# A fused retention and two-MoE kernel: the first batch's retention ordered by hand, one converted pair of weights ahead of the products

## The chip, the cores and the metric

The kernel runs on one core of a Trainium2 chip. The metric is device time in microseconds of one execution, the median of the runs shown. The engines are TensorE (PE, matrix products into PSUM), VectorE (DVE), ScalarE (ACT), GpSimd (POOL) and SyncE (SP, which issues the loads). Each works through its own queue in order.

## The reference

Three operators in a row: a retention with decay over 4 batches of 768 tokens with 8 heads of 64, a dense MLP with a squared ReLU (512 to 2048 to 512), and a mixture of 8 experts whose tokens are assigned by a greedy sort of the gate's logits. Only the first two bear on the change:

```
def _attn_ref(q, k, v):
    gamma = 1.0 - 2.0 ** (-5.0 - np.arange(H))
    for t in range(S):
        state = gamma[None, :, None, None] * state + np.einsum('bhd,bhe->bhde', k[:, :, t], v[:, :, t])
        y[:, :, t] = scale * np.einsum('bhd,bhde->bhe', q[:, :, t], state)

def _moe_ref(x, w_in, w_out, s, b):
    h = x @ w_in
    r = np.maximum(h, 0.0)
    return (s * (r * r) + b) @ w_out
```

## The kernel before

**Retention in chunks.** A chunk is 128 tokens of a batch; a batch has six (`CPB`), a block `blk` is two of them. Four tiles of a chunk are loaded (`load_chunk`: q and k by feature, k and v by token, 256 KB each) and a tile of decay factors (`load_dec`). `scale_chunk` multiplies q and v by their decays, for the first batch on POOL but for chunk 0's q. The retention of chunk j has two parts. `b_part` (here: the score step) multiplies k by q for all heads into two PSUM banks, L328, and DVE multiplies the result by the causal mask into `am`, L334. `c_part` (the value step) adds three products: `am` by v, L348, the state's update k by v, L354, and q by the state before it, L358. ACT then copies the result to `xh` (L366), DVE writes the rest to `xl` (L367), and ACT copies the state from PSUM into `Sbd` (L373), which the next chunk's value step reads. Value steps of the first four blocks write banks 5 and 2 in turn.

**High and low halves.** Every large product is made of three with operands split into a high and a low float: weights h and l, activations xh and xl, rh and rl.

**Conversion.** The dense MLP's weights come as 64-bit words. `conv_gen` turns a raw tile into a pair f of weights (its W_in part, h and l number 2f, and its W_out part, number 2f + 1), sixteen pairs in all. For a pair, ACT takes the magnitude (L237) and copies the high halves (L258), and DVE does nine operations: L248, L250, L253, L261, L263, and for both halves a subtraction L268 and an addition L270 that writes l. A raw tile is loaded two pairs ahead into one of two buffers (`conv_load`, L230), when the pair two before is done.

**Products.** For pair f and block, an h unit (`h_unit`, L415) is twelve products into bank 2 or 3 in turn; ACT takes ReLU (L418), square and high half; DVE writes the low half `rl` (L434, `low_parts`) when the next h unit is emitted. An x unit (`x_unit`, L444) is six products that add to the block's output, emitted two units behind. `moe1` runs three blocks of the first batch together: 48 h units and 48 x units in turn.

**What sets the order.** The code is emitted by hand, and each engine's queue has the order in which it is emitted. In the first stage two generators compete: `attn3` (three blocks of retention) and the conversion, by due times that the generators yield; the conversion's are stretched by `PRO` = 1.5 until pair `PN` = 2 is ready, so two pairs are ready when the products start. In the product stage `Weave` emits the product units at a fixed cost each (1,320 and 1,300) and lets the conversion go on where its due time has come: 7,100 for a pair. `conv_until(f)` emits what is missing of a pair before its first h unit.

**Then** come the retention of block 3, products of blocks 3 to 11 one after another with the next block's retention between them, and the expert stage.

Of the kernel before, what the change touches and what calls it, by code (L numbers as in the profile page):

```python
# [81 lines left out]
def kernel(  # L82
# [14 lines left out]
    x2_scratch=None,  # L97
    log_out=None,
    stages=2,
    PRO=1.5,  # L100
    PN=2,
    CY=(700, 1200, 650),
    SY=(3200, 3800, 3200, 2500, 2200, 800),
    IY=(600, 1800, 800),
# [4 lines left out]
    WARM=24,  # L109
# [65 lines left out]
    def load_chunk(j):  # L175
        if j < CPB:

            ts = []
            for i in range(4):
                n = 2 * NF - 1 - 2 * j - i // 2  # L180
                tag = ("h", "l")[i % 2] + str(n)
                ts.append(wpool.tile([128, 512], F32, name=f"first{j}_{i}", tag=tag))
            for i in (0, 1, 3, 2):
                SP.dma_start(ts[i], qkv[j, :, i])
                if j == 0 and i in first:
                    first[i]()
            if j:
                load_dec(j)
        else:
            ts = []  # L190
            load_dec(j)
            t = loads.tile([128, 4, 512], F32, name="q")
            for i in (0, 2):
                SP.dma_start(t[:, i:i + 2], qkv[j, :, i:i + 2])
                ts += [t[:, i, :], t[:, i + 1, :]]
        QKV[j] = ts

    def scale_chunk(j, q=POOL, v=POOL):
# [3 lines left out]
        if v:  # L202
# [6 lines left out]
    wb = bank(3)[:, 0:TB]  # L209
    DVE.memset(warm, 0.0)  # L210
    nv = CPB * n0
    first = {0: lambda: load_dec(0),
             1: lambda: SP.dma_start(mask_f[:, 0:128], cst[:, 128:256]),
             3: lambda: SP.dma_start(vdec, dec[:, nv:nv + CPB * H].rearrange("p (a b) -> p a b", b=H))}
    load_chunk(0)
    DVE.tensor_copy(mask, mask_f[:, 0:128])
# [15 lines left out]
    def conv_gen():  # L232
        mag = {}

        def magnitude(f):
            mag[f] = stage.tile([128, 1024], F32, name="c", tag="sa")
            ACT.activation(mag[f], RAW[f].bitcast(F32).rearrange("p (n t) -> p t n", t=2)[:, 1, :], AF.Abs)  # L237

        magnitude(0)
        for f in range(NF):  # L240
            raw = RAW.pop(f)
            (_, hi), (_, hf), (lo, _), (lf, _) = (
                [v[:, t, :] for t in range(2)] for v in
                (raw.bitcast(d).rearrange("p (n t) -> p t n", t=2) for d in (I32, F32, U32, F32)))
            c = mag.pop(f)
            ci = c.bitcast(I32)

            DVE.tensor_scalar(c, c, ZERO_WORD, None, op0=OP.max)  # L248
            yield CY[0]
            DVE.tensor_scalar(ci, ci, 3, 0x3FFFFFFF, op0=OP.logical_shift_left, op1=OP.bitwise_and)  # L250
            yield CY[0]

            DVE.scalar_tensor_tensor(hi, hi, -0x40000000, ci, op0=OP.bitwise_and, op1=OP.bitwise_or)  # L253
            for i in range(2):
                n = 2 * f + i
                W[n] = (wpool.tile([128, 512], F32R, name=f"h{n}", tag=f"h{n}"),
                        wpool.tile([128, 512], F32R, name=f"l{n}", tag=f"l{n}"))
                ACT.activation(W[n][0], hf[:, i * 512:(i + 1) * 512], AF.Copy)  # L258
            yield CY[1]

            DVE.tensor_scalar(ci, hi, -0x800000, None, op0=OP.bitwise_and)  # L261
            yield CY[0]
            DVE.scalar_tensor_tensor(lf, lo, 2.0 ** -52, c, op0=OP.mult, op1=OP.mult)  # L263
            yield CY[1]
            for i in range(2):
                h, l = W[2 * f + i]
                part = slice(i * 512, (i + 1) * 512)
                DVE.tensor_tensor(hf[:, part], hf[:, part], h.bitcast(F32), op=OP.subtract)  # L268
                yield CY[2]
                DVE.tensor_tensor(l, hf[:, part], lf[:, part], op=OP.add)  # L270
                if f + 1 < NF and not i:
                    magnitude(f + 1)
                yield CY[2]
            if f + 2 < NF:
                conv_load(f + 2)
            READY.add(f)
# [4 lines left out]
    XF = []  # L281
    pST = [None]

    def attn(blk, wide):

        if blk == NB - 1:

# [29 lines left out]
        def b_part(j):  # L317
# [17 lines left out]
                                  mask[:, None, :].to_broadcast([128, NP, 128]), op=OP.mult)  # L335
            am_of[j] = am

        def c_part(j):
            c = c0 + j
            if wide:  # L340
# [18 lines left out]
                              skip_group_check=True)  # L359
            js = slice(j * 128, (j + 1) * 128)  # L360
            yv = py.rearrange("p (a b) -> p a b", b=128)
            if blk == NB - 1:
                for i in range(2):
                    ACT.activation(XF[i][:, :, js], yv[:, 2 * i:2 * i + 2], AF.Copy, scale=scale)
            else:
                ACT.activation(xh[:, :, js], yv, AF.Copy, scale=scale)  # L366
                DVE.scalar_tensor_tensor(xl[:, :, js], yv, scale, xh[:, :, js].bitcast(F32), op0=OP.mult,  # L367
                                         op1=OP.subtract)
            if c < CPB - 1:
                pv = pST[0][:, 0:NP * 64].rearrange("p (a b) -> p a b", b=64)  # L370
                for s in range(2):
                    ss = slice(s * 64, (s + 1) * 64)
                    ACT.activation(Sbd[ss, :, ss], pv[ss], AF.Copy)  # L373
            ch = 2 * blk + j + 2
            if CPB + 2 <= ch < NC:
                load_chunk(ch)

        for j in range(2):
            if not wide:
                yield from scale_gen(j)  # L380
            yield from b_part(j)
            if wide:
                yield 1500
                if j:
                    c_part(0)
                    yield 2500
            else:
                yield 4500
                c_part(j)
                yield 9000  # L390
# [139 lines left out]
    def moe1(blks, xbs, lag, apart=0):  # L530
# [5 lines left out]
        for n in range(len(seq) + lag):  # L536
            if n < len(seq):
                def hu(n=n):
                    f, i = seq[n]
                    conv_until(f)  # L540
                    low_parts()
                    r = h_unit(blks[i], f, 2 + n % 2)
                    R2[blks[i], f] = r_split(r, work.tile([128, TB], F32R, name="rh", bufs=3),
                                             work.tile([128, TB], F32R, name="rl", bufs=3))
                units.append((1320, hu))
# [8 lines left out]
                units.append((1300, xu))  # L554
        return units

    conv_load(0)
    load_chunk(1)
    SP.dma_start(sb[:, 0:1], bass.AP(tensor=moe_s.tensor, offset=moe_s.offset, ap=[[0, 128], [1, 1]]))
    SP.dma_start(sb[:, 1:2], bass.AP(tensor=moe_b.tensor, offset=moe_b.offset, ap=[[0, 128], [1, 1]]))  # L560
    for j in range(2, CPB):
        load_chunk(j)
        if j == 3:
            conv_load(1)
    scale_chunk(0, DVE)

    def attn3():
        for b in range(3):
            yield from attn(b, True)

    a3 = Side(attn3())
    conv.due = 3000.0
    while not a3.done:
        if conv.due < a3.due and PN not in READY:
            t = conv.due
            conv.step()
            conv.due = t + PRO * (conv.due - t)
        else:
            a3.step()
    conv.due = 0.0  # L580
    wv = Weave([conv])
    for u in moe1((0, 1, 2), ((4, 5), (6, 7), (0, 1)), 2):
# [610 lines left out]
```

## Time and profile before

| | |
|---|---|
| median of 3 runs | 1068.57 us (1066.97 to 1070.48) |
| the profiled execution | 1078.43 us, its span 1076.7 us |
| PE busy | 1003.4 us, 93% of the span |
| DVE busy | 769.2 us, 71% |
| ACT busy | 462.7 us, 43% |
| POOL busy | 77.0 us, 7% |
| loads and stores | 104.48 MB, mean 97 GB/s |

The profile is of one execution on the one core. A busy share is a mean over stages with different limits, so the stages are read one by one. The granted clock is that of PE, 1.00 for the upper of its two levels (2.4 GHz) and 0.50 for the lower (1.2 GHz). A row of the timeline gives start, duration, engine, line, operation and tiles, how many in a row, and in brackets how long the engine had been idle and what ended that.

### The profile page before, as it was taken

What the parts mean: (1) busy time and instruction counts of PE and PEld (TensorE: products, weight loads), DVE (VectorE), ACT (ScalarE), POOL (GpSimd) and SP (SyncE); (2) the same over time, 40 slices, a digit from 0 to 9 for tenths busy, and PEclk for the clock granted to TensorE, in tenths of its full rate; (3) what the DMA queues carried; (4) which work ended last, traced back from release to release, by engine and by line L of the source; (5) the groups of instructions that cost most, each with busy time, mean ns of one, the idle gap of its engine ahead of it and who ended that gap; (6) DMA issues with size and microseconds to landing.
All of it is one profiled execution on the core that took longest, in us unless ns stands there. A gap on an engine that the chain in (4) does not pass through costs nothing.

```text
span 1076.7 us, 19597 instructions
## 1 busy us (share of the span) xinstructions
PE 1003.4 (93%) x7664; PEld 879.8 (82%) x7664; DVE 769.2 (71%) x1954; ACT 462.7 (43%) x1002; POOL 77.0 (7%) x99
## 2 busy tenths in 40 slices
PE   5699999899999999999998999889898988889997
PEld 4598888789899999999997987667687876768996
DVE  3799994478787787887744525869888988776431
ACT  1366664444444444344443651414433353424531
POOL 3200002000000000000000000011112021120211
PEclk8899999999999999999999999989898999999999
DMA  9234333422212121312121000522343342434430
GB/s 313 101 118 152 123 134 121 147 90 79 60 59 75 44 87 35 95 46 73 42 78 33 2 1 1 179 67 89 108 148 117 119 138 88 153 113 157 156 108 30
DMA packets 35036, 104.48 MB, mean 97 GB/s; under 512 B 4736, under 2 KB 5248, under 8 KB 34944
## 3 DMA queue, kind: packets, MB, share of 16 engines
q1 hardware_dynamic: 30528, 89.60, 25.3%
q0 software_dynamic: 3840, 12.59, 3.5%
q8 instruction: 60, 0.98, 0.4%
q10 hardware_dynamic: 576, 1.05, 0.3%
q14 instruction: 32, 0.26, 0.1%
HBM read 90.64 MB, written 12.58 MB: 96 GB/s over the span
## 4 chain that ended last, share of the span: by engine, by line
PE 65%; DVE 21%; issue 8%; DMA 2%; ACT 1%; POOL 1%; another core or an unknown queue 0%; SPq 0%; POOLq 0%; DVEq 0%; ACTq 0%
PE b L415 23%; PE b L444 18%; PE b L1023 6%; PE b L1044 4%; PE b L672 3%; DVE l L1004 3%; PE b L782 2%; PE b L348 2%; DVE big L918 2%; PE b L358 2%; DVE cmp L775 2%; PE b L328 2%; DVE hl L1032 1%; DVE raw L268 1%; DMA first<-in_qkv_dram 1%
## 5 line engine op out<-in xcount | busy, mean ns | idle before, releaser
L467 DVE SCALAR_TENSOR_TENSOR scr<-tmp,wg 128x512 bf16<-128x512 f32 x288 | 198.2, 688 | 8.8 <-ACT tmp L454 3.9
L415 PE MATMUL b<-xh,h 128*128 128x256 f32 x704 | 199.7, 284 | 1.5 <-DVE xls L367 1.4
L415 PE MATMUL b<-xl,h 128*128 128x256 f32 x704 | 199.4, 283 | 0.0
L415 PE MATMUL b<-xh,l 128*128 128x256 f32 x704 | 199.4, 283 | 0.0
L418 ACT ACTIVATE r<-b 128x256 f32<-128x256 f32 x192 | 73.3, 382 | 207.1 <-PE b L415 200.3
L415 PEld LDWEIGHTS b<-xh,h 128*128 128x128 f32 x704 | 134.7, 191 | 10.2 <-DVE xls L367 1.6
L415 PEld LDWEIGHTS b<-xl,h 128*128 128x128 f32 x704 | 134.7, 191 | 5.5
L415 PEld LDWEIGHTS b<-xh,l 128*128 128x128 f32 x704 | 134.7, 191 | 0.0
L444 PE MATMUL b<-h,rl 128*128 128x512 f32 x320 | 126.0, 394 | 3.4 <-DVE rl L434 3.4
L444 PE MATMUL b<-h,rh 128*128 128x512 f32 x320 | 128.9, 403 | 0.0
L444 PE MATMUL b<-l,rh 128*128 128x512 f32 x320 | 126.0, 394 | 0.0
L1023 PE MATMUL b<-gh,h 128*128 128x384 f32 x256 | 94.3, 368 | 9.4 <-DVE hl L1032 6.9
L434 DVE TENSOR_TENSOR rl<-r,rh 128x256 fp32r<-128x256 f32 x160 | 68.7, 430 | 46.3 <-ACT rh L427 46.0
L1023 PE MATMUL b<-gl,h 128*128 128x384 f32 x256 | 89.5, 349 | 1.5 <-DVE gl L968 1.5
L1023 PE MATMUL b<-gh,l 128*128 128x384 f32 x256 | 89.7, 351 | 0.0
L1004 DVE TENSOR_TENSOR l<-eraw,h 128x512 fp32r<-128x512 f32 x128 | 82.2, 683 | 0.0
L426 ACT ACTIVATE r<-r 128x256 f32<-128x256 f32 x192 | 79.8, 416 | 5.1
L1026 ACT ACTIVATE hh<-b 128x384 fp32r<-128x384 f32 x64 | 31.2, 488 | 117.8 <-PE b L1023 116.3
L1044 PE MATMUL b<-h,hh 128*128 128x512 f32 x192 | 79.6, 415 | 2.2 <-ACT hh L1026 2.2
L996 ACT ACTIVATE h<-eraw 128x512 fp32r<-128x512 f32 x128 | 72.7, 622 | 10.2 <-DMA eraw<-in_w_dram 9.8
L444 PEld LDWEIGHTS b<-h,rl 128*128 128x128 f32 x320 | 60.1, 188 | 20.4 <-DVE rl L434 7.1
L1044 PE MATMUL b<-h,hl 128*128 128x512 f32 x192 | 76.1, 396 | 0.4 <-DVE hl L1032 0.4
(193 smaller groups left out, 1825.4 us busy)
## 6 DMA issues: line engine op xcount, KB each, us to landing
eraw<-in_w_dram SPq DMA_DIRECT2D x64, 512.0 KB, 3.5
q<-in_qkv_dram SPq DMA_DIRECT2D x36, 512.0 KB, 4.9
raw<-in_w_dram SPq DMA_DIRECT2D x32, 512.0 KB, 4.2
first<-in_qkv_dram SPq DMA_DIRECT2D x24, 256.0 KB, 6.0
qdec<-in_dec_dram SPq DMA_DIRECT2D x24, 256.0 KB, 2.9
x2d<-tmp SPq DMA_DIRECT2D x20, 256.0 KB, 5.7
wg<-in_wgT_dram SPq DMA_DIRECT2D x4, 512.0 KB, 5.8
x2d<-tmp ACTq DMA_DIRECT2D x4, 256.0 KB, 2.3
```

The source lines that it names most:

```text
L415: PE.matmul(ph, a[:, ks], b[:, kc, :], start=(n == 0), stop=(n == 3 * KC - 1))
L418: ACT.activation(r, ph, AF.Relu)
L426: ACT.activation(r, r, AF.Square)
L434: DVE.tensor_tensor(rl, r, rh.bitcast(F32), op=OP.subtract)
L444: PE.matmul(X2[blk][t], a[:, ts], b, start=(f == 0 and i == 0), stop=(f == NF - 1 and i == 2))
L467: DVE.scalar_tensor_tensor(scr, x, 1.0, WG[e], op0=OP.mult, op1=OP.mult, accum_out=of[:, e:e + 1])
L672: PE.matmul(XB[c], a[:, cs], b, start=(f == 0 and i == 0), stop=(f == NF - 1 and i == 2))
L996: ACT.activation(hi, raw[:, a, :], AF.Copy)
L1004: DVE.tensor_tensor(lo, raw, hi.bitcast(F32), op=OP.subtract)
L1023: PE.matmul(PH[0], a[:, ks], b[:, kc, :], start=(kc == 0 and n == 0), stop=(kc == KC - 1 and n == 2))
L1026: ACT.activation(hh, PH[0], AF.Relu)
L1044: PE.matmul(Y[i, t], a[:, ts], b, start=(f == 0 and j == 0), stop=(f == NF2 - 1 and j == 2))
```

## The change

The first batch's retention is no longer given by competing generators; a loop written by hand emits it.

- The retention's body becomes a function of its own, `retention`, that returns the score and the value step. The score steps of chunks 0 and 1 come first, then for each chunk its value step, conversion steps, the score step of the chunk two ahead, more conversion steps. A table `FC` gives the number of conversion steps before and after the score step: 5 and 0, 1 and 1, 1 and 0, 1 and 0, then none. These nine are the whole of pair 0 but its end, so one pair is ready when the products start, not two; pair 1 is emitted from there on.
- Pair 1's magnitude is emitted at the end of pair 0, not within it.
- 24 filler products are added between the score steps of chunks 0 and 1.
- Loads: the decay tile is second in its chunk, not last; the first raw tile comes behind chunk 1, not before it; the second comes last, behind chunk 5.
- In the value step of blocks 0 to 3 (`wide`), the state is copied ahead of `xh`, not behind `xl`.
- h units begin with bank 3, not 2, in all blocks.

```diff
-    PRO=1.5,
-    PN=2,
+    FC=((5, 0), (1, 1), (1, 0), (1, 0), (0, 0), (0, 0)),
@@ load_chunk
             for i in (0, 1, 3, 2):
                 SP.dma_start(ts[i], qkv[j, :, i])
+                if i == 0:
+                    load_dec(j)
                 if j == 0 and i in first:
                     first[i]()
-            if j:
-                load_dec(j)
@@ conv_gen
-                if f + 1 < NF and not i:
+                if f and f + 1 < NF and not i:
                     magnitude(f + 1)
                 yield CY[2]
+            if f == 0:
+                magnitude(1)
@@ c_part
+            if wide:
+                state(c)
             if blk == NB - 1:
...
-            if c < CPB - 1:
-                pv = pST[0][:, 0:NP * 64].rearrange("p (a b) -> p a b", b=64)
-                for s in range(2):
-                    ss = slice(s * 64, (s + 1) * 64)
-                    ACT.activation(Sbd[ss, :, ss], pv[ss], AF.Copy)
+            if not wide:
+                state(c)
@@ moe1
-                    r = h_unit(blks[i], f, 2 + n % 2)
+                    r = h_unit(blks[i], f, 3 - n % 2)
@@ the first stage
+    load_chunk(1)
     conv_load(0)
-    load_chunk(1)
+    load_chunk(2)
...
-    for j in range(2, CPB):
+    for j in range(3, CPB):
         load_chunk(j)
-        if j == 3:
-            conv_load(1)
+    conv_load(1)
     scale_chunk(0, DVE)
-    def attn3():
-        for b in range(3):
-            yield from attn(b, True)
-
-    a3 = Side(attn3())
-    conv.due = 3000.0
-    while not a3.done:
-        if conv.due < a3.due and PN not in READY:
-            t = conv.due
+    rets = [retention(blk, True) for blk in range(CPB // 2)]
+
+    def scores(j):
+        for _ in rets[j // 2][1](j % 2):
+            pass
+
+    def convert(n):
+        for _ in range(n):
             conv.step()
-            conv.due = t + PRO * (conv.due - t)
-        else:
-            a3.step()
+
+    scores(0)
+    for _ in range(WARM):
+        PE.matmul(wb, warm[:, 0:128], warm, start=True, stop=True)
+    scores(1)
+    for j in range(CPB):
+        rets[j // 2][2](j % 2)
+        convert(FC[j][0])
+        if j + 2 < CPB:
+            scores(j + 2)
+        convert(FC[j][1])
     conv.due = 0.0
```

The order on the engines shows it at three places. First SP's queue behind chunk 0; firstj_0, _1, _3, _2 are chunk j's q, k, v and k by token, qdec its decay tile, raw a raw tile (two loads). Before:

```order
L230 DMA raw_135<-in_w64_dram 128x512 x2
L184 DMA first1_0_138<-in_qkv_dram 128x512
L184 DMA first1_1_139<-in_qkv_dram 128x512
L184 DMA first1_3_141<-in_qkv_dram 128x512
L184 DMA first1_2_140<-in_qkv_dram 128x512
L173 DMA qdec1_146<-in_dec_dram 128x512
```

And in the changed kernel:

```order
L183 DMA first1_0_135<-in_qkv_dram 128x512
L172 DMA qdec1_140<-in_dec_dram 128x512
L183 DMA first1_1_136<-in_qkv_dram 128x512
L183 DMA first1_3_138<-in_qkv_dram 128x512
L183 DMA first1_2_137<-in_qkv_dram 128x512
L228 DMA raw_145<-in_w64_dram 128x512 x2
```

The raw tile has moved behind chunk 1, and the decay tile to the second place.

Second, DVE's queue in the retention, from chunk 2's mask (am_301 before, am_302 now, two operations for a chunk) to chunk 3's low half; raw and c are pair 0's conversion. Before:

```order
L261 TENSOR_SCALAR c_249<-raw_135 128x1024
L263 SCALAR_TENSOR_TENSOR raw_135<-raw_135,c_249 128x1024
L334 TENSOR_TENSOR am_301<-b6_291,mask_72 128x512
L334 TENSOR_TENSOR am_301<-b7_292,mask_72 128x512
L334 TENSOR_TENSOR am_316<-b0_306,mask_72 128x512
L334 TENSOR_TENSOR am_316<-b1_307,mask_72 128x512
L268 TENSOR_TENSOR raw_135<-raw_135,h0_254 128x512
L270 TENSOR_TENSOR l0_255<-raw_135 128x512
L367 SCALAR_TENSOR_TENSOR xl_288<-b5_323,xh_287 128x4x128
```

And in the changed kernel:

```order
L246 TENSOR_SCALAR c_277<-c_277 128x1024
L248 TENSOR_SCALAR c_277<-c_277 128x1024
L251 SCALAR_TENSOR_TENSOR raw_145<-raw_145,c_277 128x1024
L259 TENSOR_SCALAR c_277<-raw_145 128x1024
L261 SCALAR_TENSOR_TENSOR raw_145<-raw_145,c_277 128x1024
L334 TENSOR_TENSOR am_302<-b6_292,mask_72 128x512
L334 TENSOR_TENSOR am_302<-b7_293,mask_72 128x512
L376 SCALAR_TENSOR_TENSOR xl_196<-b2_305,xh_195 128x4x128
L266 TENSOR_TENSOR raw_145<-raw_145,h0_282 128x512
L334 TENSOR_TENSOR am_343<-b0_333,mask_72 128x512
L334 TENSOR_TENSOR am_343<-b1_334,mask_72 128x512
L268 TENSOR_TENSOR l0_283<-raw_145 128x512
```

Five conversion operations stand together ahead of chunk 2's mask, and from there on one stands between a low half and the next mask.

Third, DVE's queue at the end of the product stage's conversions; l31 is the last low half of the weights, rl the low halves of the h units' results. Before:

```order
L263 SCALAR_TENSOR_TENSOR raw_1582<-raw_1582,c_1644 128x1024
L268 TENSOR_TENSOR raw_1582<-raw_1582,h30_1683 128x512
L434 TENSOR_TENSOR rl_1706<-r_1703,rh_1705 128x256
L270 TENSOR_TENSOR l30_1684<-raw_1582 128x512
L268 TENSOR_TENSOR raw_1582<-raw_1582,h31_1686 128x512
L270 TENSOR_TENSOR l31_1687<-raw_1582 128x512
L434 TENSOR_TENSOR rl_1735<-r_1732,rh_1734 128x256
```

And in the changed kernel:

```order
L261 SCALAR_TENSOR_TENSOR raw_1678<-raw_1678,c_1746 128x1024
L266 TENSOR_TENSOR raw_1678<-raw_1678,h30_1779 128x512
L268 TENSOR_TENSOR l30_1780<-raw_1678 128x512
L444 TENSOR_TENSOR rl_1809<-r_1806,rh_1808 128x256
L266 TENSOR_TENSOR raw_1678<-raw_1678,h31_1782 128x512
L268 TENSOR_TENSOR l31_1783<-raw_1678 128x512
L444 TENSOR_TENSOR rl_1838<-r_1835,rh_1837 128x256
```

The last rl ahead of l31 is the 38th of the stage before and the 41st now: ten h units' low halves follow l31 before, seven now. Behind this place the queues of all engines have the same order in both kernels, but for one ACT copy of `xh` in block 3.

## Rows read from the trace of the kernel before

**Rows 1.** Busy time by stretch: start:end, length, engines (instructions), PE's clock, DMA, GB/s.

```profile
7.00:54.00 47.00, 26.94 (x313) 23.58 (x313) 27.54 (x36) 12.84 (x23) 14.41 (x11) 0.78 0.58 207
...
102.00:167.80 65.80, 63.64 (x395) 54.66 (x393) 64.25 (x95) 42.03 (x91) 3.29 (x2) 1.00 0.40 137
```

**Rows 2.** The chain of waits, 0 to 62 us: start, duration, what.

```profile
43.78 1.23 DVE raw L253
```

**Rows 3.** Timeline of PE, 0 to 60 us: score, value and first h products.

```profile
7.06 1.16 PE L328 MATMUL b<-first,first 64*128 64x128 f32 x16 [0.69 <-DVE first L201]
...
16.10 2.08 PE L328 MATMUL b<-first,first 64*128 64x128 f32 x16 [7.87 <-DMA first<-in_qkv_dram]
...
18.11 1.97 PE L348 MATMUL b<-am,first 128*64 128x128 f32 x16
...
20.45 1.04 PE L348 MATMUL b<-am,first 128*64 128x128 f32 x16
...
21.56 0.69 PE L354 MATMUL b<-first,first 128*64 128x64 f32 x16
...
39.91 1.16 PE L358 MATMUL b<-first,sbd 128*128 128x128 f32 x8
...
45.67 0.43 PE L348 MATMUL b<-am,first 128*64 128x128 f32 x2 [2.62 <-DVE am L334]
...
47.99 2.08 PE L358 MATMUL b<-first,sbd 128*128 128x128 f32 x8
...
54.00 0.39 PE L415 MATMUL b<-xh,h 128*128 128x256 f32 x1 [1.41 <-DVE xls L367]
```

**Rows 4.** The chain of waits, 160 to 196 us.

```profile
166.52 1.19 DVE rl L434
...
168.95 1.42 PE b L415 x12
170.37 1.39 PE b L444 x6
...
194.22 1.14 PE b L328 x16
```

**Rows 5.** Timeline of DVE in the product stage: first and fourteenth pair's start, an rl.

```profile
55.19 0.69 DVE L248 TENSOR_SCALAR c<-c 128x1024 f32<-128x1024 f32 x1
...
59.26 0.42 DVE L434 TENSOR_TENSOR rl<-r,rh 128x256 fp32r<-128x256 f32 x1
...
159.95 0.69 DVE L248 TENSOR_SCALAR c<-c 128x1024 f32<-128x1024 f32 x1
```

**Rows 6.** Timeline of POOL, 0 to 40 us: scaling of chunks 1, 2 and 3.

```profile
14.79 1.26 POOL L201 TENSOR_TENSOR first<-first,qdec 128x512 f32<-128x512 f32 x1 [6.58 <-DMA qdec<-in_dec_dram]
...
19.46 1.27 POOL L201 TENSOR_TENSOR first<-first,qdec 128x512 f32<-128x512 f32 x1 [2.41 <-DMA qdec<-in_dec_dram]
...
23.04 1.49 POOL L201 TENSOR_TENSOR first<-first,qdec 128x512 f32<-128x512 f32 x1 [1.31 <-DMA qdec<-in_dec_dram]
```

**Rows 7.** Timeline of ACT and DVE, 0 to 60 us: copies, conversion operations, masks.

```profile
21.53 1.15 ACT L237 ACTIVATE c<-raw 128x1024 f32<-128x1024 f32 x1
...
23.44 1.64 DVE L250 TENSOR_SCALAR c<-c 128x1024 int32<-128x1024 int32 x1
...
25.12 1.95 DVE L253 SCALAR_TENSOR_TENSOR raw<-raw,c 128x1024 int32<-128x1024 int32 x1
...
30.28 2.17 DVE L263 SCALAR_TENSOR_TENSOR raw<-raw,c 128x1024 f32<-128x1024 uint32 x1
...
37.98 0.60 ACT L366 ACTIVATE xh<-b 128x512 fp32r<-128x512 f32 x1 [7.19 <-PE b L358]
38.47 0.77 ACT L373 ACTIVATE sbd<-b 64x256 f32<-64x256 f32 x2
...
44.93 2.48 DVE L334 TENSOR_TENSOR am<-b,mask 128x512 f32<-128x512 f32 x4
```

**Rows 8.** Raw tiles' loads in the product stage, issue to landing.

```profile
DMA to landing us min/median/max: 3.4/3.6/4.7
```

More of the change, by code (lines that the diff above doesn't have):

```diff
@@ L211 @@
     nv = CPB * n0
-    first = {0: lambda: load_dec(0),
-             1: lambda: SP.dma_start(mask_f[:, 0:128], cst[:, 128:256]),
+    first = {1: lambda: SP.dma_start(mask_f[:, 0:128], cst[:, 128:256]),
              3: lambda: SP.dma_start(vdec, dec[:, nv:nv + CPB * H].rearrange("p (a b) -> p a b", b=H))}
@@ L282, with retention @@
     pST = [None]
-    def attn(blk, wide):
+    def retention(blk, wide):
         if blk == NB - 1:
@@ L336, in b_part, with state @@
             am_of[j] = am
+        def state(c):
+            if c < CPB - 1:
+                pv = pST[0][:, 0:NP * 64].rearrange("p (a b) -> p a b", b=64)
+                for s in range(2):
+                    ss = slice(s * 64, (s + 1) * 64)
+                    ACT.activation(Sbd[ss, :, ss], pv[ss], AF.Copy)
         def c_part(j):
@@ L376, in c_part, with attn @@
                 load_chunk(ch)
+        return scale_gen, b_part, c_part
+    def attn(blk, wide):
+        scale_gen, b_part, c_part = retention(blk, wide)
         for j in range(2):
```

## The prediction

> **What bounds the kernel now.** The table by stretches comes first [rows 1]. From 7 to 54 us, where the first batch's retention runs, TensorE (PE) is busy 26.94 of 47.00 us at a mean granted clock of 0.78, and VectorE (DVE) 27.54: nothing is full, so latencies rule. From 102.0 to 167.8, in the product stage, DVE is busy 64.25 of 65.80 us: there DVE is the bound. The chain of waits of the first 62 us [rows 2] shows what the latencies are: conversion operations on DVE (43.78), and then the masks that stand behind them in its queue. The first product of the next stage, at 54.00, waited 1.41 us for DVE's low half xls [rows 3]. The chain of the product stage [rows 4] runs over DVE until the subtraction rl ends at 167.71, then over PE without a gap to 194.22. So the end of the stage is the start of DVE's conversions in it, plus DVE's work up to that rl, plus the products left then. One h unit takes 1.43 us and one x unit 1.39 [rows 4]; a pair of units 2.82.
>
> Below, S(j) are the score products of chunk j, V(j) its three value products, T_P is the start of the first h unit (54.00 before), T_D that of the first conversion operation DVE does after the last retention step (55.19 before [rows 5]).
>
> **Loads.** SP's queue gives bytes at fixed places: before, the decay tiles of chunks 1, 2 and 3 end at 3.76, 5.07 and 6.38 MB, and the scaling on POOL that waits for them starts at 14.79, 19.46 and 23.04 us [rows 6]. Now each decay tile stands second in its chunk and the first raw pair behind chunk 1: chunk 1's ends at 1.92 MB, chunk 2's at 4.28, chunk 3's at 5.60, the raw pair at 3.76. Between those marks (2.7 to 3.6 us for a MB) this gives about 10 us (half of the bytes that were there at 14.79), 16.7, 20.9, and 14.8 for the raw pair; on the same slope chunk 4's comes at 24.5 and chunk 5's at 28. These are estimates from the three rows.
>
> **Retention by hand.** S(0) is where it was (7.06 [rows 3]). The added 24 fillers cost 24 x 0.119 = 2.9 us at the upper clock level (an h unit is twelve such products in 1.43 us [rows 4]), 5.7 at the lower; they cover PE's wait for chunk 1, which is scaled at 10 + 1.3 = 11.3. I take the upper level, since PE has been busy until then, so they cost nothing; at the lower one S(1) starts near 13.9 and what hangs on V(0) slips by 3 us. S(1) and V(0) end near 14.3; the state copy, now ahead of xh, takes 0.77 and xh 0.60 on ACT, magnitude 1.15 [rows 7]: 16.9. Then five conversion operations stand on DVE ahead of the mask of S(2): 0.69 + 0.69 + 1.23 + 0.68 + 1.23 = 4.5 us when alone (1.23 in [rows 2], 0.69 in [rows 5]; 0.68 and 0.69 are one kind). POOL scales chunks 2 and 3 in that time, and beside POOL three of these took 1.64, 1.95 and 2.17 [rows 7], 2.6 us more. So the mask, four times 0.62 for two chunks [rows 7], is done at 22.7 or 25.3. I take 25.3, because the scaling falls on the same operations.
>
> On PE, S(2) waits for the scaled chunk 2: 16.7 + 1.4 = 18.1. PE has then idled 3.8 us. Before, an idle of 2.62 us was followed by a fall of the granted clock (45.67, and 2.08 instead of 1.16 us for a state product at 47.99), and after the idle of 7.87 the products at 16.10 and 18.11 ran at the lower of the two levels, 4 us in all, before 1.04 and 0.69 at the upper [rows 3]. Taking the same: S(2) 2.08, V(1) 1.97 + 0.69 + 1.16, S(3) 1.16, to 25.2; at the upper level throughout 23.5. From there PE is the longest queue: V(2) 2.9, S(4) 1.16, V(3) 2.9, S(5) 1.16, V(4) 2.9, V(5) 2.2 = 13.2. The masks keep ahead of it: xl(2) starts 1.4 us after V(2), with one conversion step and the mask it ends 4.1 us after, and V(4) starts 5.2 us after. So T_P = 25.3 + 13.2 = 38.5, with the ends 36.7 (upper level, no POOL beside DVE: 23.5 + 13.2) and 41.5 (fillers at the lower level).
>
> That DVE's operations grow beside POOL by about one POOL instruction (0.72 to 0.95 us against 1.04 to 1.27) is in [rows 6, 7]. The Trainium skill, "SBUF — State Buffer", section "Who interferes with whom", says that the port pair that VectorE and GpSimd share is locked for a whole instruction and the later one blocks fully. The trace agrees. It speaks against this change, since it puts the conversion among the scalings: if by that rule all five operations each waited out one POOL instruction, 5 x 1.15 = 5.8 us would stand where the sum has 2.6, T_P would be 41.7 and the time 1057.2 instead of 1054.0.
>
> **The bank swap.** The first h unit now writes bank 3. Before, it waited for xls, which reads bank 2, for 1.41 us [rows 3]. The gain is already in T_P, which follows V(5) directly.
>
> **Only one pair ahead.** T_D follows xhs (0.60) and the moved magnitude (1.15): T_D = 38.5 + 1.8 = 40.3. The second pair's first half needs nine operations, 4.5 + 0.69 + 0.69 and two rl of 0.42 [rows 5]: 6.7 us, to T_P + 8.5. PE wants it at T_P + 3 x 1.43 + 1.39 = 5.7, and two of the twelve products go ahead: a stall of about 2.6 us that before did not have. It sets the end only if PE does. The loads behind it are no later than before: raw takes 3.4 to 4.7 us to land [rows 8], and the magnitude that uses it comes 6 us after its issue.
>
> **The end of the product stage.** From 55.19 to 167.71 DVE did fourteen pairs but for the last three operations, with rl 0 to 37: 112.5 us. Fourteen starts of a pair, 55.19 to 159.95, give 8.06 us for a pair with its rl [rows 5]. The changed order has one pair more, but the pacing of a pair (7,100 against 7,860 for three units) also lets three more rl into the queue: the rl before the last low half is the 41st instead of the 38th. So 112.5 + 8.1 + 0.6 (one operation more ahead of it) = 121.2, and 40.3 + 121.2 = 161.5. What PE has left was 194.22 - 167.75 = 26.5, now three pairs less: 26.5 - 8.5 = 18.0. End at 179.5. By PE alone it would be 38.5 + 48 x 2.82 + 2.6 = 176.5, so DVE still sets it. Saved: 194.2 - 179.5 = 14.7 us. Behind it every queue has the order it had, but for a state copy ahead of one xh on ACT; the next step there waits for a load. The profiled execution takes 1078.43 us (span 1076.7), the median of the runs 1068.57, a ratio of 0.991: 14.6 us, 1054.0.
>
> **Rivals.**
> A, shorter retention: no lower clock level and no POOL beside DVE, T_P 36.7. 16.5 us saved, 1052.2. For it: PE is denser than before. Against: the 3.8 us idle.
> B, the lower clock level lasts until S(4), since the bursts are small: 18.1 + 2.08 + 5.3 + 2.08 + 5.3 + 2.08 + 9.2 = 44.2 (V is 1.97 + 2 x 0.69 + 2.08 there). 9.0 us saved, 1059.6. For it: the mean of 0.78 [rows 1]. Against: from 20.45 on it was up again after 4 us [rows 3].
> C, the extra pair is not repaid: the last rl that PE waits for is still followed by 26.5 us of products. 14.7 - 8.5 = 6.2, 1062.4. Against: the order has 41 rl there.
> D, the change doesn't do what it says: PE stays at the lower level through the retention, nine steps of S and V take 33.7 us instead of 18.4, T_P = 51.8. Saved 1.4 us, 1067.2.
> E, slower: with one pair in hand each pair waits for its raw tile. DVE would need over 8.06 + 14.7 / 15 = 9.04 us for a pair to lose; with a landing of 8 us after the release (8 + 0.45 + 1.15 = 9.6) the fifteen pairs lose 23 us, 1076.9. For it: the buffer against such waits is halved. Against: no landing of the product stage took over 4.7 us [rows 8].
>
> **How the numbers follow.** Forecast (T_P 37.5 to 40.8, 1053.0 to 1056.3) 0.50, A 0.18, B 0.15, C 0.06, D 0.05, E 0.06. The range takes A and nearly all of B with the forecast: 1050.5 to 1060.0; C, D and E are left out. Within 0.3% (3.2 us, about what a measurement of this kernel tells from no change) only D falls: faster 0.89, same 0.05, slower 0.06.
>
> **What would show it.** The first h unit at 37 to 41 us; masks of S(2) behind five conversion operations; a lower clock in the stretch from 18 to 22 only; the fourth h unit's stall of 2 to 3 us; DVE full until about 161 and PE without gaps from there to 179 or 180; the rest shifted by the same 14 to 15 us. It is wrong if the products start after 43, if DVE waits for raw tiles, or if PE has over 20 us of products left when DVE's conversions end.

## The result, and the profile after

The changed kernel takes 1055.62 us (median of 4 runs, 1054.47 to 1057.85) against 1069.11 for the kernel before (median of 4): a ratio of 0.9878 with a 95% interval of 0.9855 to 0.9902, or 13.0 us less (10.5 to 15.5). The forecast was 1054.0, the range 1050.5 to 1060.0.

| mark in the profiled execution, us | before | forecast | after |
|---|---|---|---|
| first h unit, T_P | 54.00 | 38.5 | 38.76 |
| first conversion operation after retention, T_D | 55.19 | 40.3 | 40.70 |
| last rl that PE waits for ends | 167.71 | 161.5 | 161.89 |
| products left from there | 26.5 | 18.0 | 18.0 |
| end of the stage | 194.22 | 179.5 | 179.94 |

The stage ends 14.28 us earlier, where 14.7 were forecast. At the last score step of the product stages, at 571.55 us before and 557.05 after, the profile of after is 14.5 us ahead. From that step to the end of its span the profile of before takes 505.2 us and that of after 496.8. The change is not what makes this difference: among the experiments below, this stretch takes 503 to 508 us in every profile from one chip (e1 to e8) and 495.0 to 495.3 in every one from another (e9 to e12), whatever was edited. So the profile of before seems to come from a chip like the first and that of after from one like the second; no run here confirms it. What stands behind that step is not compared. The forecast's step from 14.7 to 14.6, by the ratio of median to profiled time, spread that difference over all stages. It changed 0.1 us and nothing else.

The stretches of after, with the columns of [rows 1]:

```profile
7.00:40.00 33.00, 26.78 (x346) 23.84 (x347) 20.54 (x27) 11.30 (x21) 15.16 (x11) 0.95 0.84 294
...
88.00:152.00 64.00, 63.61 (x400) 56.23 (x400) 62.43 (x96) 42.38 (x90) 0.00 (x0) 1.00 0.39 136
```

Retention now fills 7 to 39 us instead of 7 to 54. PE is busy for 26.78 us, fillers included, against 26.94, but in 33 us rather than 47, at a granted clock of 0.95 rather than 0.78. DVE has 20.54 us there rather than 27.54: the second pair's operations have left the stretch. In the product stage DVE is as full as before (62.43 of 64.00 us against 64.25 of 65.80), and PE a little fuller (63.61 of 64.00 against 63.64 of 65.80).

The timeline of after, 7 to 43 us, cut to the places that answer [rows 3, 5, 6, 7] (start, duration, engine, line, tile; idle time before it and its releaser in brackets):

```profile
7.98 2.79 PE L590 MATMUL b<-rh 128*128 128x256 bf16 x24
...
10.23 1.26 POOL L200 TENSOR_TENSOR first<-first,qdec 128x512 f32<-128x512 f32 x1 [1.92 <-DMA qdec<-in_dec_dram]
...
14.35 1.28 ACT L343 ACT_TABLE_LOAD   x1 [14.35 <-PE b L361]
16.90 1.27 POOL L200 TENSOR_TENSOR first<-first,qdec 128x512 f32<-128x512 f32 x1 [3.60 <-DMA qdec<-in_dec_dram]
16.95 1.14 ACT L235 ACTIVATE c<-raw 128x1024 f32<-128x1024 f32 x1
...
18.11 0.69 DVE L246 TENSOR_SCALAR c<-c 128x1024 f32<-128x1024 f32 x1 [0.34 <-ACT c L235]
18.14 1.57 POOL L203 TENSOR_TENSOR first<-first,vdec 128x512 f32<-128x512 f32 x1
...
18.23 1.66 PE L328 MATMUL b<-first,first 64*128 64x128 f32 x16 [3.97 <-POOL first L200]
18.84 1.42 DVE L248 TENSOR_SCALAR c<-c 128x1024 int32<-128x1024 int32 x1
...
20.29 1.23 DVE L251 SCALAR_TENSOR_TENSOR raw<-raw,c 128x1024 int32<-128x1024 int32 x1
20.32 2.33 POOL L200 TENSOR_TENSOR first<-first,qdec 128x512 f32<-128x512 f32 x1 [0.61 <-DMA qdec<-in_dec_dram]
...
21.55 1.66 DVE L259 TENSOR_SCALAR c<-raw 128x1024 int32<-128x1024 int32 x1
...
22.77 1.34 POOL L203 TENSOR_TENSOR first<-first,vdec 128x512 f32<-128x512 f32 x1
...
23.25 1.96 DVE L261 SCALAR_TENSOR_TENSOR raw<-raw,c 128x1024 f32<-128x1024 uint32 x1
...
25.11 1.28 DVE L334 TENSOR_TENSOR am<-b,mask 128x512 f32<-128x512 f32 x2
...
25.85 0.43 PE L355 MATMUL b<-am,first 128*64 128x128 f32 x2 [1.20 <-DVE am L334]
...
26.45 0.98 PE L355 MATMUL b<-am,first 128*64 128x128 f32 x13 [0.17 <-DVE am L334]
...
29.02 1.16 PE L328 MATMUL b<-first,first 64*128 64x128 f32 x16
...
32.69 1.16 PE L328 MATMUL b<-first,first 64*128 64x128 f32 x16
...
38.76 0.36 PE L425 MATMUL b<-xh,h 128*128 128x256 f32 x1
...
40.70 0.69 DVE L246 TENSOR_SCALAR c<-c 128x1024 f32<-128x1024 f32 x1 [0.33 <-ACT c L235]
...
42.03 0.42 DVE L444 TENSOR_TENSOR rl<-r,rh 128x256 fp32r<-128x256 f32 x1
```

Read it downwards: the fillers, 2.79 us, then chunk 1 scaled at 10.23 where [rows 6] had 14.79, and chunks 2 and 3 at 16.90 and 20.32 where it had 19.46 and 23.04. S(2) waits 3.97 us for chunk 2 and runs partly at the lower clock level (1.66 us; 1.16 at the upper, 2.08 at the lower). The mask of S(2) comes at 25.11, behind five conversion operations of which three are long (1.42, 1.66, 1.96). From 25.85 PE runs almost without a gap to the first h unit, which no longer waits for xls. One line was not in the forecast: ACT loads its function table at 14.35, between V(0) and the state copy.

The chain of waits of after at the end of the stage, against [rows 4]:

```profile
161.47 0.42 DVE rl L444
...
161.93 1.19 PE b L454 x4
163.12 1.43 PE b L425 x12
...
179.94 1.14 PE b L328 x16
```

It still goes over DVE to an rl and then over PE alone, from 161.93 to 179.94.

### The profile page after: what moved, and what is told of

It reads as the page before. It is cut to its first block, busy times and chain, and to the rows that moved or that the text cites. A ratio compares the mean times of both kernels' runs of the same rounds, so it can differ in the third digit from the quotient of the medians.

```text
span 1053.8 us, 19655 instructions
## 1 busy us (share of the span) xinstructions
PE 998.0 (95%) x7688; PEld 876.4 (83%) x7688; DVE 769.4 (73%) x1954; ACT 464.5 (44%) x1002; POOL 77.0 (7%) x99
## 4 chain that ended last, share of the span: by engine, by line
PE 66%; DVE 21%; issue 9%; ACT 2%; POOL 1%; DMA 1%; SPq 0%; POOLq 0%; DVEq 0%; ACTq 0%
PE b L425 22%; PE b L454 17%; PE b L1041 6%; PE b L1062 5%; PE b L690 4%; DVE l L1022 3%; PE b L800 2%; DVE big L936 2%; PE b L328 2%; PE b L355 2%; PE b L365 2%; DVE cmp L793 1%; DVE raw L266 1%; DVE raw L251 1%; DVE rl L444 1%
## 5 line engine op out<-in xcount | busy, mean ns | idle before, releaser
L444 DVE TENSOR_TENSOR rl<-r,rh 128x256 fp32r<-128x256 f32 x160 | 68.2, 427 | 38.5 <-ACT rh L437 38.4
L1062 PE MATMUL b<-l,hh 128*128 128x512 f32 x192 | 75.8, 395 | 0.0
```

The costliest lines, as they stand in the source:

```text
L444: DVE.tensor_tensor(rl, r, rh.bitcast(F32), op=OP.subtract)
L1062: PE.matmul(Y[i, t], a[:, ts], b, start=(f == 0 and j == 0), stop=(f == NF2 - 1 and j == 2))
```

## The experiments

T_P is again the start of the first h unit. E is the start of the first score product of the next block, by the timeline: 194.15 before, 179.87 after. Behind T_P lie E - T_P = 140.1 us before and 141.1 after. Ratios are against the kernel before on the same chip as the run; its medians were 1076.2 and 1077.8 us on one chip and 1069.8 on the other. Of the parts of the change, the state copy ahead of `xh` and the moved magnitude have no run of their own.

**e1_one_pair: one pair ahead, alone.** The kernel before, with its generators told to convert one pair instead of two ahead of the products. (They stop when the pair numbered `PN`, counted from 0, is ready; in the kernel before the retention ended first, with two pairs ready.)

```diff
-    PN=2,
+    PN=0,
```

> The kernel before with one edit: its generators stop the conversion once pair 0 is ready, so one pair is ahead of the products; retention order, loads and banks are those of before. Theory (end = start of DVE's conversions in the product stage + its work + the products left then): in the retention two conversion operations leave DVE ahead of the masks of chunks 4 and 5, PE's idle of 2.62 us there shrinks to about 1.3, the first h unit starts near 51 (54.00 before), and the stage ends near 189.5 (194.22): some 5 us of the 14.3 that the whole change saves. Rival (a pair not converted early is converted late): the first h unit starts earlier, but the end stays at 194, within 0.7 us.

Measured: T_P 52.26, E 192.34, E - T_P 140.1 as before; ratio 0.9995 (0.998 to 1.001). The mask that V(4) waits for came sooner, a wait of 0.63 us where [rows 3] has 2.62 at 45.67. PE's timeline of this run:

```profile
45.10 0.43 PE L348 MATMUL b<-am,first 128*64 128x128 f32 x2 [0.63 <-DVE am L334]
```

So in this execution the pair that is now converted in the product stage costs nothing at the stage's end, and taking it out of the retention gives back 1.7 us there; neither the 5 of the one theory nor the 0 of the other. The times of the runs don't tell 1.7 us from no change. Of the 15.2 us by which the retention gets shorter, fewer operations on DVE are at most a small part.

**e2_no_swap: the banks of the first h units as before.**

```diff
-                    r = h_unit(blks[i], f, 3 - n % 2)
+                    r = h_unit(blks[i], f, 2 + n % 2)
```

> The changed kernel with the banks of the h units in the old order (bank 2 first). The first h unit then waits for the last retention step's xls, which ends at 40.37 in the changed kernel: it starts at 40.4 instead of 38.76. Theory (DVE sets the end): DVE's conversions start at 40.7 as before, and the stage's end stays at 179.9, at most 0.5 later. Rival (PE sets the end): 1.6 later, 181.5.

Measured: T_P 40.06, after a wait of 1.41 us for xls as before; E 181.00; ratio 0.9906 (0.9889 to 0.9922). T_D did not move later (40.33), yet the end came 1.1 us later. I had expected the end unchanged, because DVE sets it and DVE's start was the same. That fell. DVE's timeline of this run shows why:

```profile
41.06 0.69 DVE L248 TENSOR_SCALAR c<-c 128x1024 int32<-128x1024 int32 x1
43.10 0.42 DVE L444 TENSOR_TENSOR rl<-r,rh 128x256 fp32r<-128x256 f32 x1 [1.35 <-ACT rh L437]
```

Two operations into the stage DVE comes to the first rl, which needs the first h unit through ACT, and stands still for 1.35 us; in after it came to it at 42.03 without a wait. The first rl ties DVE's queue to T_P.

**e3_old_loads and e12_loads_only: the two halves of the change.** The first is the changed kernel with the loads of before, the second the kernel before with the new order of loads. Their diffs are one the reverse of the other:

```diff
+    load_chunk(1)
     conv_load(0)
-    load_chunk(1)
+    load_chunk(2)
...
-    for j in range(2, CPB):
+    for j in range(3, CPB):
         load_chunk(j)
-        if j == 3:
-            conv_load(1)
+    conv_load(1)
```

with each decay tile second in its chunk, as in the change. (These lines are e12's.)

> The changed kernel with the load order of before (first raw tile ahead of chunk 1, decay tiles last in their chunks, second raw tile behind chunk 3). Theory: chunk 1's scaling starts at 14.8 instead of 10.2, so the score step of chunk 1, the value step of chunk 0, the magnitude and the five conversion operations ahead of chunk 2's mask all come 4 to 7 us later; first h unit at 43 to 46 (38.76), the end later by the same. Rival (the loads matter only where chunk 2 is waited for, 19.5 instead of 16.9): 2.6 us later, first h unit at 41.4.

> The kernel before with the new load order only (decay tile second, first raw tile behind chunk 1, second raw tile last); its generators and banks stay. Theory (loads and the order by hand work together: undoing the loads cost the changed kernel 7.8 us, but the old order holds the masks behind pair 1's conversion and runs at the lower clock level): the first h unit at 49 to 53 instead of 54.0, the end 1 to 5 us earlier. Rival (the loads alone are worth their 7.8 us): first h unit at 46, end at 186.4.

Measured: e3 has T_P 46.54 and E 187.67, ratio 0.9954 (0.9935 to 0.9972). The timeline of e3_old_loads:

```profile
14.57 1.26 POOL L200 TENSOR_TENSOR first<-first,qdec 128x512 f32<-128x512 f32 x1 [6.50 <-DMA qdec<-in_dec_dram]
15.88 2.08 PE L329 MATMUL b<-first,first 64*128 64x128 f32 x16 [5.04 <-POOL first L200]
...
31.28 2.35 PE L356 MATMUL b<-am,first 128*64 128x128 f32 x15 [3.55 <-DVE am L335]
```

Chunk 1 is scaled where it was before the change [rows 6]; PE idles 5.04 us and is at the lower level behind it (granted clock 0.51 from 15 to 20 us). Later it idles 3.55 more for a mask, and a second stretch at the lower level follows (0.50 from 28 to 36 us): the 15 products of V(2) take 2.35 us, in after 1.58, from 25.85 to 27.43. That is 7.8 us against the 4 to 7 expected, and the gain of the hand order without the loads is 54.0 - 46.5 = 7.5.

e12 has T_P 50.76 and E 190.90, ratio 0.9953 (0.9937 to 0.9969): 3.2 us, inside the 1 to 5 of the theory. The timeline of e12_loads_only:

```profile
33.41 1.12 ACT L236 ACTIVATE c<-raw 128x1024 f32<-128x1024 f32 x1 [9.60 <-DMA raw<-in_w_dram]
35.05 0.77 ACT L372 ACTIVATE sbd<-b 64x256 f32<-64x256 f32 x2
35.87 1.12 PE L353 MATMUL b<-first,first 128*64 128x64 f32 x16 [3.04 <-ACT sbd L372]
```

The new order loads the second raw pair last. In the old order of the work ACT reaches that pair's magnitude in the middle of the retention, waits 9.60 us for it, and holds the state copy behind it, for which PE then waits. So the halves need each other: 3.2 alone and 7.5 alone, but 54.00 - 38.76 = 15.2 together. (By the ratios it is 5.0, 4.9 and 13.0 us; their intervals, some 2 us to each side, don't tell 9.9 from 13.0. So that the halves need each other is shown in single executions only, with the row of ACT's 9.60 us for the mechanism.)

**e4_pace: a longer pacing of the conversion.** The changed kernel with each pace 8% longer, so that a pair is spread over more units.

```diff
-    CY=(700, 1200, 650),
+    CY=(756, 1296, 702),
```

> The changed kernel with the conversion's due times stretched by 1.08 (7,668 for a pair instead of 7,100, against 7,860 for the three units that use it), so that the rl stand further ahead in DVE's queue. Theory (in the second half PE waits for rl that stand behind conversions not needed yet): these waits go, the stage ends where PE alone would end, 177 to 178 instead of 179.9. Rival (DVE is simply full): 179.9 or later, with new waits of h units for low halves of the weights.

Measured: T_P 39.32, E 179.24, E - T_P 139.9, ratio 0.9871 (0.9852 to 0.9889). The waits of PE, 35 to 200 us, by tile and releaser (sum, count, longest), first of after:

```profile
PE b L425 <- DVE l L268: 2.0, 1, 2.0
PE b L454 <- DVE rl L444: 1.7, 2, 1.4
```

and of e4_pace, where the second line has gone:

```profile
PE b L425 <- DVE l L268: 2.9, 2, 2.0
```

PE's waits for rl went, but only 1.2 us of the expected 2 to 3 came back behind T_P: a part turned into waits for low halves. The ratio is that of the changed kernel.

**e5_table: ACT's table load out of the way.** The changed kernel with a one-element activation at its start.

```diff
     DVE.memset(warm, 0.0)
+    pre = consts.tile([128, 1], F32, name="pre")
+    DVE.memset(pre, 0.0)
+    ACT.activation(pre, pre, AF.Copy)
```

> The changed kernel with one tiny ACT copy at the start, so that ACT's table load (1.28 us at 14.35 in the changed kernel, between the value step of chunk 0 and the first state copy) is over before it is needed. Theory (the load lies on the path that runs over the state copy, xh, the magnitude and the five conversion operations to chunk 2's mask): first h unit and stage end 1.1 to 1.4 us earlier (37.5, 178.6). Rival (POOL's scaling beside DVE sets that mask anyway): under 0.4.

Measured: the magnitude starts at 15.65 instead of 16.95, but the mask of S(2) starts at 24.74, 0.4 earlier and not 1.2. Begun earlier, four of the five conversion operations run beside POOL's scalings (1.64, 1.95, 1.65, 1.95 us). T_P is 38.39. E is 181.02, 1.15 later than after; ratio 0.9893 (0.9874 to 0.9911). So the table load is worth 0.4 us here at most, not 1.3; in e9, with no edit at all, that mask starts at 24.86. Where the 1.5 us behind T_P went is told at e9.

**e6_ahead: four operations more before the products**, against the stall of the fourth h unit.

```diff
-    FC=((5, 0), (1, 1), (1, 0), (1, 0), (0, 0), (0, 0)),
+    FC=((5, 0), (1, 1), (1, 0), (1, 1), (1, 1), (1, 0)),
```

> The changed kernel with four more conversion steps in the retention (table (5,0), (1,1), (1,0), (1,1), (1,1), (1,0)), in holes that DVE has between the last masks and low halves. Theory (from the first rl on DVE and PE run locked, and only one pair ahead costs the fourth h unit's stall of 2.0 to 2.2 us): the first h unit starts where it did (38.8, within 0.5), the stall on the second pair's low half goes, the stage ends 2 to 3 us earlier (177 to 178). Rival (what is converted early only moves, as with one pair less in the kernel before): the end stays within 0.7 of 179.9.

Measured: T_P 38.21, E 181.26, ratio 0.9879 (0.9856 to 0.9901). The wait for the second pair's low half is gone, and a new one stands in PE's waits:

```profile
PE b L425 <- DVE xls L376: 2.6, 1, 2.6
```

The operations put ahead delay DVE's last low half of the retention through ACT: its high copies of the second pair (39.99), which need them, now stand before its last xhs, which starts at 41.10 and not at 39.05 as in after. The wait moved, with nothing gained.

**e7_no_fill: without the 24 fillers.**

```diff
     scores(0)
-    for _ in range(WARM):
-        PE.matmul(wb, warm[:, 0:128], warm, start=True, stop=True)
     scores(1)
```

> The changed kernel without the 24 fillers. Theory (PE idles 3.5 us ahead of chunk 1's scores and the clock falls): scores of chunk 1 and the value step of chunk 0 take 2.08 and about 3.3 us instead of 1.16 and 1.7, chunk 2's mask and the first h unit come 1.5 to 2.5 us later. Rival (the clock has fallen by chunk 2's scores in any case, and the mask of chunk 2 waits for conversions): the first h unit moves by under 0.5 us.

Measured: in the profiled execution T_P 43.69 and E 184.81. Its PE timeline:

```profile
11.62 2.08 PE L328 MATMUL b<-first,first 64*128 64x128 f32 x16 [3.62 <-DMA first<-in_qkv_dram]
13.62 1.97 PE L355 MATMUL b<-am,first 128*64 128x128 f32 x16
...
28.39 2.35 PE L355 MATMUL b<-am,first 128*64 128x128 f32 x15 [5.37 <-DVE am L334]
```

S(1) and V(0) now run at the lower level: the granted clock of 12 to 16 us is 0.50. After the later wait of 5.37 us for the mask (1.20 in after) it fell to 0.50 a second time, for 28 to 33 us. That is 4.9 us more than after, where 1.5 to 2.5 were expected. But this was the slowest of the kernel's four runs (1063.85 to 1067.54), and the ratio, 0.9882 (0.9861 to 0.9902), is that of the changed kernel. What the fillers are worth over many executions stays open; the trace only shows the fall that they prevent in S(1).

**e8_no_port: POOL idle beside the conversion.** The changed kernel leaves out the scaling of chunk 2's value and of chunk 3 on POOL; nothing does it instead.

> The changed kernel without the scaling of chunk 2's v and of chunk 3's q and v on POOL (left out, nothing does it instead); chunk 2's q is still scaled, so its scores start as before. Theory (DVE's conversion operations grow because POOL holds the port pair): the operations that took 1.42, 1.66 and 1.96 us take 0.69, 0.69 and 1.23, the mask of chunk 2 starts at 22.5 instead of 25.1, chunk 2's value step then follows the scores of chunk 3 without a wait, first h unit 1.2 to 1.6 us earlier. Rival (the loads slow DVE): durations stay.

Measured in one execution: T_P 36.86 and the mask of S(2) 3.0 us earlier, 0.6 of them because the conversion began at 17.52 and not at 18.11. The DVE timeline of e8_no_port:

```profile
18.25 0.69 DVE L251 TENSOR_SCALAR c<-c 128x1024 int32<-128x1024 int32 x1
...
20.23 0.69 DVE L262 TENSOR_SCALAR c<-raw 128x1024 int32<-128x1024 int32 x1
20.96 1.23 DVE L264 SCALAR_TENSOR_TENSOR raw<-raw,c 128x1024 f32<-128x1024 uint32 x1
22.11 1.28 DVE L337 TENSOR_TENSOR am<-b,mask 128x512 f32<-128x512 f32 x2
```

The three operations that take 1.42, 1.66 and 1.96 us in after take 0.69, 0.69 and 1.23. With POOL idle the growth is gone; it was POOL. T_P is 1.9 us earlier than in after and 1.65 us earlier than in e9 (expected: 1.2 to 1.6). PE's timeline of this run has S(2) at the lower level still:

```profile
17.40 2.08 PE L331 MATMUL b<-first,first 64*128 64x128 f32 x16 [3.74 <-POOL first L203]
```

E (179.51) shows little of it, again because of what e9 shows.

**e9_same: the changed kernel once more.** No edit.

> The changed kernel once more, unedited, on one chip with the three others. Theory (a PE wait of 2 us or more is sometimes followed by the lower clock level, so first h unit and stage end scatter between executions): first h unit 38 to 40.5, stage end 141 to 142.7 after it, ratio 0.985 to 0.990. Rival (both are fixed by the order): 38.8 and 179.9 within 0.3.

Measured: ratio 0.9875 (0.9858 to 0.9892), the median 1056.0. T_P 38.51, but E 181.17: 1.3 us later than in the first profile of the same kernel. At the last score step this profile is 2.7 us behind the first, so 11.8 us ahead of before where the first is 14.5; the 13.0 us by the times of the runs lie between. PE's stretches (length, busy, granted clock, DMA) of the first profile, after:

```profile
45.00:48.00 3.00, 1.02 (x9) 1.00 0.00 0
48.00:51.00 3.00, 3.00 (x22) 1.00 0.51 145
```

and of e9_same:

```profile
45.00:48.00 3.00, 1.07 (x5) 0.83 0.00 0
48.00:51.00 3.00, 3.00 (x13) 0.60 0.58 162
```

Both idle 2 us for the second pair's low half. In the one the clock stays at 2.4 GHz, in the other it falls behind the idle, and the units there take up to twice as long. In e5_table it was so too:

```profile
48.00:51.00 3.00, 3.00 (x11) 0.53 0.65 187
```

E - T_P sorts by it: 142.6, 142.65, 143.05 and 142.7 us in e5, e8, e6 and e9, where a clock of 0.53 to 0.75 stands in some stretch of 42 to 51 us, and 141.1, 140.9, 141.1, 139.9, 141.1, 141.6 and 138.6 in after, e2, e3, e4, e7, e10 and e11, where it is 1.00 from 42 to 60. So the marks of single executions of this kernel scatter by about 1.5 us, and differences of that size behind T_P (e4, e5, e6, e8) can't be put down to the edit; e2's 1.1 us is believed for its wait on DVE, not for its size.

**e10_no_stall: the stall of the fourth h unit by two changes at once.** Two operations more before the products, and the first step of the conversion due later.

```diff
-    FC=((5, 0), (1, 1), (1, 0), (1, 0), (0, 0), (0, 0)),
+    FC=((5, 0), (1, 1), (1, 0), (1, 1), (1, 0), (0, 0)),
...
-    conv.due = 0.0
+    conv.due = 1000.0
```

> The changed kernel with two more conversion steps in the retention (table (5,0), (1,1), (1,0), (1,1), (1,0), (0,0)) and the conversion's first due time in the product stage at 1,000 instead of 0, so that pair 1's high halves stand behind the first ReLU on ACT. Theory: the fourth h unit's wait falls from 2.0 to about 0.9 us, no lower clock level follows, the stage ends 1 to 2 us less after the first h unit (139 to 140 instead of 141.1). Rival (DVE full from the first rl on sets the end whatever stands ahead): 141 as before, the wait moves to rl.

Measured: T_P 38.25, E 179.82, ratio 0.9878 (0.9859 to 0.9897); the stall is still 1.9 us. The timeline of e10_no_stall:

```profile
41.15 1.23 ACT L256 ACTIVATE h<-raw 128x512 fp32r<-128x512 f32 x2
...
43.58 0.42 DVE L444 TENSOR_TENSOR rl<-r,rh 128x256 fp32r<-128x256 f32 x1 [1.28 <-ACT rh L437]
```

With the conversion further on, ACT's high copies come earlier, ahead of the second h unit's work; DVE waits 1.28 us for that unit's rh and loses what was won. Neither more operations ahead (e6) nor these two edits bring a gain: one wait goes or shrinks and another comes, since DVE needs rh from ACT there and ACT needs DVE's operations for its high copies.

**e11_all: e10, e5's early activation and e4's pacing together.**

```diff
+    FC=((5, 0), (1, 1), (1, 0), (1, 1), (1, 0), (0, 0)),
+    CY=(756, 1296, 702),
...
+    ACT.activation(pre, pre, AF.Copy)
...
+    conv.due = 1000.0
```

> The kernel of e10_no_stall with the early table load of e5_table and the due times of e4_pace: the three edits together, a candidate that should beat both kernels. Theory: first h unit 37.5 to 38.8, stage end 138 to 139 after it, 176 to 177.5; 2.5 to 4 us less than the changed kernel, ratio 0.982 to 0.986 where the changed kernel has 0.987. Rival (the three act on one wait): as e10_no_stall.

Measured: the lowest median of the study, 1054.48 us (1052.04 to 1055.38), ratio 0.9859 (0.984 to 0.9878), against 1056.0 for the unedited kernel on the same chip. The two intervals overlap, so it isn't told apart from the changed kernel. E - T_P is 138.6, as expected, but T_P is 39.67 instead of 37.5 to 38.8: with the conversion earlier, POOL is the one that is held. The timeline of e11_all:

```profile
17.63 2.29 POOL L200 TENSOR_TENSOR first<-first,qdec 128x512 f32<-128x512 f32 x1 [5.13 <-DMA qdec<-in_dec_dram]
...
19.98 2.08 PE L331 MATMUL b<-first,first 64*128 64x128 f32 x16 [6.43 <-POOL first L200]
```

Chunk 2's scaling starts 0.7 us later than in after, when its decay tile has landed, and takes 2.29 us instead of 1.27. S(2) waits for it until 19.98 and runs at the lower level.

## Why the prediction was right, step by step

**The bound.** Right: latencies up to T_P, DVE behind it up to the last waited rl, PE alone for the rest. T_P came out 0.3 us later than forecast, the end 0.4.

**Loads.** The scalings were put at 10, 16.7, 20.9, 24.5 and 28 from three rows; they start at 10.23, 16.90, 20.32, 25.71 and 28.97. Right within 1.2 us, and e3 shows what hangs on it: 7.8 us.

**Retention.** Two terms were off and cancelled, 1.1 us too little and 0.9 too much: that T_P came out within 0.3 us is in part luck. The table load, 1.28 us on ACT ahead of the state copy, was missing: the conversion began at 18.11 instead of 16.9, and the mask of S(2) ended at 26.4 instead of 25.3. Still, it is not a term by itself: in e5, without it there, the five operations grew by 7.88 - 4.5 = 3.4 us instead of 2.4, and the mask gained 0.4 at most. That the load would come just there could not be seen in [rows 7], since in the kernel before it lay at 0.76 us, where ACT had nothing else to do. The Trainium skill, "ScalarE: Activation LUTs", section "What ACT_TABLE_LOAD costs", gives 1283 ns for such a load; the row has 1.28. Against that, PE's series from V(2) to T_P took 38.76 - 26.45 = 12.3 us instead of 13.2: I had added durations of groups, whose rows overlap, while a score and a value step follow each other every 3.67 us (29.02 to 32.69) and not every 4.06. The growth beside POOL was right: 0.73 + 0.97 + 0.73 = 2.4 us against 2.6, and e8 shows that POOL is its cause. The Trainium skill, "SBUF — State Buffer", section "Who interferes with whom", has the shared port pair locked for a whole instruction, and the issue order deciding who is held; the traces agree, also in that the held one can be POOL (2.33 us at 20.32, 2.29 in e11). That all five operations would wait, T_P 41.7, did not happen: two of the five took 0.69 and 1.23 as when alone. These two had begun just before POOL's next instruction (18.11 against 18.14, 20.29 against 20.32), and there POOL grew, to 1.57 from 1.04 and to 2.33. The three long ones began while POOL was at work (18.84, 21.55 and 23.25) and end 0.5 to 1.1 us after its instruction.

**The lower clock.** Expected from S(2) to 22 us. It was there, but shorter: S(2) took 1.66 us instead of 2.08. What the fillers cost was right (2.79 us, all under a wait); what they are worth was not priced at all, and the one trace without them shows S(1) and V(0) at the lower level.

**The bank swap.** Its 1.41 us was counted in T_P, and that held (e2: T_P 1.3 later). But the step from there, "the end of the stage is the start of DVE's conversions in it, plus DVE's work", was incomplete: in e2 T_D stayed and the end still moved by 1.1. DVE's queue holds rl early, and rl follows T_P. In the forecast T_P and T_D moved together, so the gap didn't show.

**Only one pair ahead.** The stall was 2.0 us instead of 2.6. The extra pair was repaid: 18.0 us of products left as forecast, and e1 with the same E - T_P as before. For the retention itself the missing pair is worth 1.7 us in that one execution.

**The rivals.** A (16.5 us saved) needed both the upper level and POOL idle. With POOL idle alone e8 comes to its number, 36.86 against 36.7, but not by its mechanism: S(2) takes 2.08 us at the lower level there, and PE's series is shorter than the sum had it. B's lower level up to S(4) did not come: 29.02 and 32.69 are 1.16 us long. C fell with the 18.0 us, and D with T_P. E did not come: raw tiles took up to 6.0 us to land, not 4.7 as in [rows 8], but between 35 and 170 us ACT waited for them four times, 1.5 us in all, and DVE never directly. Two sums among the rivals are slightly off: at the upper level S(3) ends at 23.3, not 23.5, and B's value step is 5.43, not 5.3. Nothing hangs on them.

## What to carry to other kernels

An order of loads and an order of work are one change: here 3.2 us and 7.5 us alone, 15.2 together at the first h unit of single executions, because what is loaded last must also be asked for last, on every queue that stands in between. To forecast such an edit, follow one queue to the last operation that someone waits for, add what the other engine has left then, and look for the operations by which that queue depends on the other engine's start. Before an effect under 2 us is believed from a trace, profile the unedited kernel twice.

## What was not expected of the hardware

- In after, ACT's table load stands behind the first activation's wait, at 14.35 us; in before it ran at 0.76, though the first activation waited until 20.13. What decides was not found. An early activation of one element per partition brings it to 0.76 (e5).
- After the same 2 us wait of PE the granted clock stayed at 1.00 in one execution and fell to 0.60 in another of the same kernel, with the end of the stage about 1.5 us later, counted from the first h unit. What decides between them was not found.
- DVE and POOL hold each other, the later one being held: beside each other 0.69 became 1.42 and 1.66, 1.23 became 1.96 us on DVE, and 1.27 became 2.29 to 2.33 on POOL.
